# An attention kernel whose instruction order comes from a plan: refitted step lengths, a price for each pair of matmul forms, a narrower hold on VectorE, and a new order of TensorE's steps

## The chip, the cores and the metric

The kernel runs on one core of one Trainium2 chip. The metric is the device time of one execution in microseconds (us), the median over several runs. The profile calls TensorE PE (and its weight loads PEld), VectorE DVE, ScalarE ACT, GpSimd POOL and SyncE SP; a q behind a name (SPq) is the engine's queue of issued transfers.

## The reference: what is computed

Two stages in fp32. The first is attention inside chunks of 64 positions, for 8 batches, 8 heads and 576 positions. The second takes its output as x (8 batches of 576 x 512) and runs four experts, each a causal attention of width 64 over the whole sequence, of which each position uses the best two by a gate.

```
scores = scale * q_c @ k_c.T ; attn = softmax(scores) ; x = attn @ v_c     # chunks of 64
logits = x @ w_gate ; keep the 2 largest of 4, softmax over them -> w
for e in range(4):
    q, k, v = x @ wq[e], x @ wk[e], x @ wv[e]
    a = softmax(causal(scale * q @ k.T))                                    # 576 x 576
    ye = a @ v @ wo[e]
    out += w[e] * ye                                                        # for the positions that chose e
```

## The kernel before, in words

The work is cut into steps, and every step has a name, a number and an engine. A file-wide function builds them all as a graph: `add` (L85) records one step with its engine, its supposed length, what it depends on and which buffers it uses. Nothing is issued while the graph is built. Then `Plan.emit` (L142) walks through time on the host, engine by engine, with the supposed lengths, and issues each step's instructions in the order in which the walk starts them. So the lengths in the code never run on the chip; they only decide the order in which each engine's instructions stand. On the chip each engine then takes its instructions strictly in that order and waits by semaphores for data and buffers.

**TensorE's steps** are not chosen by the walk but by the table `ORDER` (L269): 372 names. They are, for the first stage, `as` (scores of a unit of one or two groups of 128 positions, L510), `at` (transposes of its softmax, L549) and `av` (times v, L570); there are 22 units. For the second stage `v` (the value projection and gate of one group, L461) and `m` (a query or key projection of one tile of 256 or 384 positions, L461; `m` 4t and 4t+1 are the queries of the two expert pairs of tile t, 4t+2 and 4t+3 the keys), `s` (scores of one row tile of one batch and expert pair, L712; `s1.2` is the third of the six steps of batch 0, pair 1), `st` (transposes of the weights, L786), `o` (weights times values, L820) and `w` (output projection of 128 positions, L850). The first four `m` and first two `v` are split into two parts, `m2` and `m2.1` being the high-order product and the two correction products. A step has one of four forms by the part of TensorE's array that its matmuls use, which the profile shows as 128*128 ("full": m, v, w), 64*128 ("rows": s, st, at), 64*64 ("quarters": as, av) and 128*64 ("cols": o).

**The other engines' steps** are taken by the walk from those that can start, the one with the smallest due time first. The due time comes from TensorE's order and is shifted by the tables `LATER` (L286, one shift per kind and engine) and `MOVED` (L293, one shift per single step). ScalarE takes the exponentials (`aa` L529, `sa` L729), copies out of PSUM (`ac` L557, `sc` L800), the high parts of x, q and k (`ax` L592, `za` L627), the values (`va` L490), half of the outputs (`y` L861) and the high parts of the weight matrices (`wh` L442). VectorE takes maxima, differences and sums of the first softmax (`ad` L520 to L535), the low parts (`ay` L594, `zd` L632 and L634), the masked scores (`sd` L722) and others. GpSimd normalises the first softmax (`ap` L538), forms the low parts of the weight matrices (`wl` L446), computes the gate and scales the second softmax (`sp` L753). SyncE issues the transfers: `lq` (K and Q of a group, L404 and L405), `lv` (V, L408), `lw` (a piece of a weight matrix, L439) and `so` (an output, L859). The very first Q goes from ScalarE's queue.

Buffers are few: 8 PSUM banks; 4 each of the K, Q and V groups; 2 each of `e` (the first softmax of a unit), `et` and `mx`; 4 of `at` (the weights of the second softmax), 2 of x.

The walk knows four things of TensorE beside a step's length: a price for a change of form (`CHANGE`, L54, by the new form alone), a stall when a new block of instructions is fetched (`fetched`, L150), a slower start (L324) and a number of filler matmuls (L325). It also knows that some VectorE and GpSimd steps get in each other's way: a VectorE step marked `port=True` is held while GpSimd is busy or has a step whose inputs are ready:

```
if held and eng == "DVE":
    if free_at["Pool"] > now or any(a.ready <= now for a in avail["Pool"]):
        continue
```

## Time and profile before

| | us |
|---|---|
| median of 3 runs | 386.13 |
| lowest and highest run | 386.06, 388.39 |
| the profiled execution | 386.02 |
| its span, first to last instruction | 384.3 |
| first matmul of a step | 4.40 |
| first matmul of av0 | 14.05 |

The granted TensorE clock is 1.0 in the profile. The views used are the page's busy times, the table of stretches (busy time of each engine in each stretch), the table of waits (who waited for whom, longest first in total, then the number of waits and the longest), the timeline (start, length, engine, line, operation, output from inputs, count; in brackets the idle time before it and what ended it) and the chain of work that ended last, in order of time (start, length, what). PE counts as busy from a matmul's start to its modelled end, so overlapping matmuls are counted once, and a weight load (PEld) can stand idle while PE is still busy.

### The profile page before, as it was taken

To read this page: it belongs to the slowest core of one execution; us is meant where nothing else is said; L and a number is where in the kernel's file an instruction comes from. 1 tells how busy PE (TensorE), PEld (TensorE's weight loads), DVE (VectorE), ACT (ScalarE), POOL (GpSimd) and SP (SyncE) were. 2 spreads that over 40 slices of the span, in tenths; PEclk is the share of its full clock that TensorE was granted. 3 is DMA by queue.
4 is the path that set the end of the run, shared out by engine and by line. 5 is a ranking of instruction groups with operands and counts; after the bars stand their busy time and mean duration, and the time that the engine had idled before them with its cause. 6 is when DMAs were issued, how large, how long until landed. Compare 5 with 4: busy or idle time off the path is not lost.

```text
span 384.3 us, 14186 instructions
## 1 busy us (share of the span) xinstructions
PE 374.5 (97%) x5602; PEld 330.2 (86%) x5603; DVE 272.1 (71%) x946; ACT 270.3 (70%) x890; POOL 170.7 (44%) x335
## 2 busy tenths in 40 slices
PE   6799999999999999999999999999999999999996
PEld 4699999898989899797997989988989889897674
DVE  3667899999489795888436779776755766668531
ACT  3564799789746965979744496798494765969651
POOL 6653255657163069455160205763705046166700
PEclk9999999999999999999999999999999999999999
DMA  8954532605252270414106126003100110000224
GB/s 286 380 200 181 195 96 78 217 3 148 77 184 93 90 245 28 163 61 139 57 29 197 53 68 239 29 3 128 67 17 15 30 58 1 2 29 3 110 84 164
DMA packets 22098, 40.76 MB, mean 106 GB/s; under 512 B 2448, under 2 KB 2704, under 8 KB 22032
## 3 DMA queue, kind: packets, MB, share of 16 engines
q1 hardware_dynamic: 21744, 39.47, 29.8%
q8 instruction: 44, 0.72, 0.8%
q10 hardware_dynamic: 288, 0.39, 0.3%
q14 instruction: 22, 0.18, 0.1%
HBM read 30.42 MB, written 9.44 MB: 104 GB/s over the span
## 4 chain that ended last, share of the span: by engine, by line
PE 92%; DMA 3%; DVE 2%; ACT 1%; issue 1%; POOL 1%; SPq 0%; POOLq 0%
PE bank L461 39%; PE bank L850 14%; PE bank L820 12%; PE bank L712 11%; PE bank L786 6%; PE bank L570 5%; PE bank L510 4%; PE bank L549 2%; DMA at<-in_wqk_dram 2%; DMA qs<-in_qt_dram 1%; POOL e L538 1%; DVE xl L594 0%; DVE e L522 0%; DVE mx L520 0%; ACT e L529 0%
## 5 line engine op out<-in xcount | busy, mean ns | idle before, releaser
L753 POOL TENSOR_SCALAR at<-at,st,gate 128x320 f32<-128x320 f32 (+4 forms) x160 | 95.0, 611 | 74.5 <-DVE st L743 49.0
L729 ACT ACTIVATE at<-at,st 128x448 f32<-128x448 f32 (+4 forms) x160 | 90.0, 601 | 0.1
L722 DVE CUSTOM_DVE_ANT_0 at<-bank,mask 128x448 f32<-128x448 f32 (+4 forms) x160 | 60.0, 425 | 12.2 <-PE bank L712 11.4
L461 PE MATMUL bank<-xh,wqk_hi 128*128 128x384 f32 (+1 forms) x208 | 65.5, 326 | 0.0
L461 PE MATMUL bank<-xl,wqk_hi 128*128 128x384 f32 (+1 forms) x208 | 65.2, 323 | 0.0
L461 PE MATMUL bank<-xh,wqk_lo 128*128 128x384 f32 (+1 forms) x208 | 65.1, 323 | 0.0
L800 ACT ACTIVATE aT<-bank 128x128 f32<-128x128 f32 (+2 forms) x256 | 57.0, 377 | 2.4 <-PE bank L786 2.0
L538 POOL TENSOR_TENSOR e<-e,mx 128x1024 f32<-128x1024 f32 (+1 forms) x21 | 34.3, 1645 | 50.1 <-DVE mx L535 28.3
L820 PE MATMUL bank<-aT,vv 128*64 128x448 f32 (+4 forms) x384 | 46.7, 392 | 0.0
L820 PEld LDWEIGHTS bank<-aT,vv 128*64 128x64 f32 x384 | 25.0, 137 | 21.8 <-issue 15.2
L764 DVE STREAM_TRANSPOSE aT<-at 32x96 f32<-32x96 f32 x128 | 34.5, 269 | 12.5 <-POOL at L753 9.0
L461 PE MATMUL bank<-wvg_hi,xh 128*128 128x260 f32 x144 | 40.5, 288 | 0.0
L461 PE MATMUL bank<-wvg_lo,xh 128*128 128x260 f32 x144 | 39.7, 283 | 0.0
L461 PE MATMUL bank<-wvg_hi,xl 128*128 128x260 f32 x144 | 39.5, 281 | 0.0
L461 PEld LDWEIGHTS bank<-xh,wqk_hi 128*128 128x128 f32 x208 | 38.2, 188 | 0.8
L461 PEld LDWEIGHTS bank<-xl,wqk_hi 128*128 128x128 f32 x208 | 38.4, 188 | 0.5 <-DVE xl L594 0.2
L461 PEld LDWEIGHTS bank<-xh,wqk_lo 128*128 128x128 f32 x208 | 38.3, 188 | 0.0
L729 ACT ACTIVATION_READ_ACCUMULATOR at<-at,st 128x1 f32 (+1 forms) x160 | 38.1, 239 | 0.0
L712 PE MATMUL bank<-kh,qh 64*128 64x288 f32 (+4 forms) x192 | 37.1, 338 | 0.0
L490 ACT ACTIVATE vv<-bank 64x260 f32<-64x260 f32 (+1 forms) x56 | 21.6, 385 | 22.0 <-PE bank L461 21.6
L712 PE MATMUL bank<-kl,qh 64*128 64x288 f32 (+4 forms) x192 | 32.8, 294 | 0.0
L786 PEld LDWEIGHTS bank<-ident,at 64*128 64x128 f32 x704 | 28.9, 139 | 3.8 <-issue 1.5
(91 smaller groups left out, 822.4 us busy)
## 6 DMA issues: line engine op xcount, KB each, us to landing
ks<-in_kt_dram SPq DMA_DIRECT2D x36, 256.0 KB, 4.7
vs<-in_vt_dram SPq DMA_DIRECT2D x36, 256.0 KB, 4.1
qs<-in_qt_dram SPq DMA_DIRECT2D x35, 256.0 KB, 5.0
out_dram<-y SPq DMA_DIRECT2D x35, 256.0 KB, 2.0
at<-in_wqk_dram SPq DMA_DIRECT2D x4, 256.0 KB, 6.4
at<-in_wvg_dram SPq DMA_DIRECT2D x2, 260.0 KB, 4.3
at<-in_wo_dram SPq DMA_DIRECT2D x2, 256.0 KB, 5.7
qs<-in_qt_dram ACTq DMA_DIRECT2D x1, 256.0 KB, 3.6
```

Of the source, the lines that this page charges most:

```text
L461: pe.matmul(bk.t[:, :n_], a, x, start=(n == 0), stop=(n == 3 * KT - 1))
L490: act.activation(v_s[b].t[p0:p0 + m, j], bk.t[r0:r0 + m, 0:W_VG], AF.Copy)
L538: o = add("DVE" if u in NORM_DVE else "Pool", 0.6 if u in NORM_DVE else 0.14 + 0.87 * G, lambda: norm.tensor_tensor(e.t[:, al], e.t[:, al] ...
L712: pe.matmul(bks[s].t[:m, :w], q[own, cs], k[own, z0 + ks.start:z0 + ks.stop], start=(x == 0), stop=(x == 2))
L722: dve.tensor_tensor_reduce(out=a.t[:r, o_ + ks.start:o_ + ks.stop], in0=bk.t[:r, :w], in1=mask[:r, m0:m0 + w], scale=1.0, scalar=first, op ...
L729: act.activation(af, af, AF.Exp, scale=-1.0, bias=st.t[:r, 0, i, 0:1], accum_out=st.t[:r, 1, i, 0:1])
L753: pool.tensor_scalar(af, af, st.t[:r, 2, i, 0:1], gt.t[:r, i, e:e + 1], op0=OP.mult, op1=OP.mult)
L764: dve.transpose(dst, src)
L786: pe.transpose(bks[r].t[:, 64 * n:64 * n + 64], a.t[own, c0:c0 + 128], ident[own, own])
L800: act.activation(dst, bks[r].t[:, n:n + 64 * m].rearrange("p (j c) -> p j c", j=m), AF.Copy)
L820: pe.matmul(bk.t[64 * s:64 * s + 64, c0 - h0:h1 - h0], vs.t[:, j, 64 * (2 * pair + s):64 * (2 * pair + s) + 64], ts[s].t[:, 448 * j + c0:4 ...
L850: pe.matmul(bk.t, up[:, k, 128 * t:128 * t + 128], wp[:, k, :], start=(n == 0), stop=(n == 5))
```

## The change

Five things are changed, all of them in the plan; no instruction is added, removed or given another shape, except that the same 372 steps stand in another order.

- `CHANGE` prices each pair of old and new form.
- The supposed lengths of TensorE's steps and of the transfers are refitted (`SCORES`, `TURNS` and single numbers).
- VectorE's step with `port=True` is held only if GpSimd is busy or has a step that could begin now, its buffers included; the test on the buffers is moved into a function `fits`.
- `ORDER` is another permutation of the 372 names. By the forms above it changes form 82 times, before 78: from full to quarters 4 (before 2), from quarters to full 9 (8), from quarters to cols 8 (7), from rows to full 6 (5), from rows to cols 6 (7), the others as before.
- `LATER` and `MOVED` have other numbers for most entries.

```
-CHANGE = {"rows": 0.15, "quarters": 0.135, "cols": 0.17, "full": 0.2}
+CHANGE = {("full", "rows"): 0.13, ("full", "quarters"): 0.133, ("full", "cols"): 0.14, ("rows", "full"): 0.236,
+          ("rows", "quarters"): 0.157, ("rows", "cols"): 0.182, ("quarters", "full"): 0.22, ("quarters", "rows"): 0.16,
+          ("quarters", "cols"): 0.16, ("cols", "full"): 0.206, ("cols", "rows"): 0.133, ("cols", "quarters"): 0.146}
...
+        def fits(o):
+            need = {}
+            for u in o.uses:
+                if u.t is None:
+                    need[id(u.pool)] = (u.pool, need.get(id(u.pool), (None, 0))[1] + 1)
+            return all(len(p) >= n for p, n in need.values())
...
-                    if free_at["Pool"] > now or any(a.ready <= now for a in avail["Pool"]):
+                    if free_at["Pool"] > now or any(a.ready <= now and fits(a) for a in avail["Pool"]):
...
-                    dur += CHANGE[o.form] if o.form != state["form"] else 0.0
+                    dur += CHANGE.get((state["form"], o.form), 0.0)
...
-as0 as1 at0 at1 av0 as3 av1 as2 v0 m1 m0 v0.1 m2 m3 v1 m3.1 m0.1 v1.1 m2.1 m1.1 at3 at2 as4 av3 av2 as5 v3 v2 m4 m6
-m7 m5 at4 at5 s0.3 av4 as6 av5 v4 m11 m10 m8 v6 s1 s0 s0.1 s0.4 s1.1 at6 s0.5 s0.2 as7 av6 v5 m9 v8 m14 st1 s1.4 st3
+as0 as1 at0 at1 av0 as2 as3 av1 v0 m2 m3 v1 m2.1 m1 m0 m1.1 m3.1 v0.1 m0.1 at2 s1.1 at3 v1.1 av2 av3 as5 as4 v2 v3
+m5 m6 m4 m7 s0.2 at4 at5 s1.2 av4 as6 av5 as9 v4 m11 v5 m8 m10 s0.1 s0.4 s0.3 at6 s0.5 s1.3 s0 as7 av6 v6 m9 m12 m14
...
-    "lw2@SP": 33.35, "lw4@SP": -61.14, "wh4@ACT": 1.19, "lw5@SP": -8.53, "wh5@ACT": -5.21, "lw6@SP": 0.21,
+    "lw2@SP": 3.31, "wh2@ACT": -1.68, "wl2@Pool": 2.15, "wh3@ACT": 9.23, "wl3@Pool": 0.2, "lw4@SP": -0.41,
...
-SCORES = {64: 0.205, 192: 0.397, 288: 0.402, 320: 0.483, 448: 0.61}
-TURNS = (0.249, 0.43)
+SCORES = {64: 0.196, 192: 0.417, 288: 0.478, 320: 0.522, 448: 0.669}
+TURNS = (0.246, 0.423)
...
-        kq_op[g] = add("dma", {0: 0.73}.get(g, 1.3), lambda: None, deps=[a], uses=[q_s[g], k_s[g]])
+        kq_op[g] = add("dma", {0: 0.73, 2: 2.4}.get(g, 1.37), lambda: None, deps=[a], uses=[q_s[g], k_s[g]])
```

Since tables of numbers set the order, three places are shown as the two built programs have them. In the new file a line's number is one higher.

The first is ScalarE at the start, from its first activation on. `wvg_hi` and `wqk_hi` are high parts of weight matrices, `e_81` and `e_82` the softmaxes of units 0 and 1, `et` copies of their transposes, `xh` the high part of x. Before:

```order
L442 ACTIVATE wvg_hi<-at_101 128x520
L529 ACTIVATE e_81<-e_81 128x256 x2
L442 ACTIVATE wvg_hi<-at_101 128x520
L529 ACTIVATE e_82<-e_82 128x256 x2
L442 ACTIVATE wqk_hi<-at_102 128x512
L442 ACTIVATE wqk_hi<-at_103 128x512
L442 ACTIVATE wqk_hi<-at_102 128x512
L557 ACTIVATE et_83<-bank_65 128x256
L557 ACTIVATE et_84<-bank_67 128x256
L592 ACTIVATE xh_87<-bank_61 128x2x128
```

Now:

```order
L443 ACTIVATE wvg_hi<-at_101 128x520
L530 ACTIVATE e_81<-e_81 128x256
L443 ACTIVATE wvg_hi<-at_101 128x520
L530 ACTIVATE e_81<-e_81 128x256
L530 ACTIVATE e_82<-e_82 128x256 x2
L443 ACTIVATE wqk_hi<-at_102 128x512
L443 ACTIVATE wqk_hi<-at_103 128x512
L558 ACTIVATE et_83<-bank_65 128x256
L443 ACTIVATE wqk_hi<-at_103 128x512
L558 ACTIVATE et_84<-bank_67 128x256
L593 ACTIVATE xh_87<-bank_62 128x2x128
```

The copy `et_83`, for which av0 waits, now stands behind two pieces of `wqk_hi` instead of three; the second half of unit 0's exponentials stands behind the second piece of `wvg_hi`.

The second is SyncE's queue at the start, from its first transfer. Before:

```order
L404 DMA ks_73<-in_kt_dram 128x512
L439 DMA at_101<-in_wvg_dram 128x520
L404 DMA ks_74<-in_kt_dram 128x512
L405 DMA qs_70<-in_qt_dram 128x512
L408 DMA vs_77<-in_vt_dram 128x512
L439 DMA at_101<-in_wvg_dram 128x520
```

Now:

```order
L440 DMA at_101<-in_wvg_dram 128x520
L405 DMA ks_73<-in_kt_dram 128x512
L409 DMA vs_77<-in_vt_dram 128x512
L405 DMA ks_74<-in_kt_dram 128x512
L406 DMA qs_70<-in_qt_dram 128x512
L440 DMA at_101<-in_wvg_dram 128x520
```

The first K (ks_73) is now issued second, and the K and Q of group 1 (ks_74, qs_70) fourth and fifth instead of third and fourth.

The third is GpSimd where it first scales the second softmax (`at`) and then normalises the next unit's first softmax (`e`). Before:

```order
L753 TENSOR_SCALAR at_102<-at_102,st_108,gate_114 128x448
L753 TENSOR_SCALAR at_102<-at_102,st_108,gate_114 128x320
L753 TENSOR_SCALAR at_102<-at_102,st_108,gate_114 128x192
L753 TENSOR_SCALAR at_102<-at_102,st_108,gate_114 64x64
L538 TENSOR_TENSOR e_82<-e_82,mx_85 128x1024
L753 TENSOR_SCALAR at_103<-at_103,st_109,gate_114 128x320
```

Now:

```order
L754 TENSOR_SCALAR at_104<-at_104,st_110,gate_114 64x64
L754 TENSOR_SCALAR at_104<-at_104,st_110,gate_114 128x576
L754 TENSOR_SCALAR at_104<-at_104,st_110,gate_114 128x448
L539 TENSOR_TENSOR e_81<-e_81,mx_85 128x512
L539 TENSOR_TENSOR e_82<-e_82,mx_86 128x1024
L754 TENSOR_SCALAR at_101<-at_101,st_107,gate_114 128x320
```

Unit 9 (the 512 wide one) now comes before unit 7 (1024 wide), because as9 now stands 13 places ahead of as7 in `ORDER` (before, 17 behind it). From there to at9, 21 places behind at8, unit 9 holds one of the two `e` buffers.

More of the change, by code (lines that the diff above doesn't have):

```diff
@@ L194, in emit @@
                         continue
-                    need = {}
-                    for u in o.uses:
-                        if u.t is None:
-                            need[id(u.pool)] = (u.pool, need.get(id(u.pool), (None, 0))[1] + 1)
-                    if any(len(p) < n for p, n in need.values()):
+                    if not fits(o):
                         continue
@@ L269 @@
 ORDER = """
-as0 as1 at0 at1 av0 as3 av1 as2 v0 m1 m0 v0.1 m2 m3 v1 m3.1 m0.1 v1.1 m2.1 m1.1 at3 at2 as4 av3 av2 as5 v3 v2 m4 m6
-m7 m5 at4 at5 s0.3 av4 as6 av5 v4 m11 m10 m8 v6 s1 s0 s0.1 s0.4 s1.1 at6 s0.5 s0.2 as7 av6 v5 m9 v8 m14 st1 s1.4 st3
-s1.2 st2 s1.3 st0 at7 s1.5 s3 as8 as9 av7 o0 m15 m13 m12 v7 s3.4 st4 st5 s3.5 st7 s3.1 s3.3 st6 s3.2 at9 at8 s2.4
-s2.5 s2.1 s2.2 s2.3 o1 av8 av9 as10 w0 m19 v10 v11 v9 m17 s2 st14 st13 st15 at10 st12 m16 m18 as11 av10 as12 o3 v12
-m21 m23 m20 st8 st9 s5.1 s5 at12 s5.4 st10 s5.2 st11 s5.5 s4.2 at11 s5.3 o2 av11 as16 as13 v13 v14 w4 m22 w3 w2 v17
@@ new lines @@
+m5 m6 m4 m7 s0.2 at4 at5 s1.2 av4 as6 av5 as9 v4 m11 v5 m8 m10 s0.1 s0.4 s0.3 at6 s0.5 s1.3 s0 as7 av6 v6 m9 m12 m14
+v8 st1 s1 st0 s1.4 st2 s1.5 st3 at7 s3.1 as8 o0 m13 m15 v7 s3 st4 st5 s3.4 st6 s3.3 st7 s3.2 at8 s2.4 s3.5 s2.1 s2.5
+o1 av8 av7 as10 w1 v12 m17 m19 v10 st12 st13 s2 s2.3 st14 s2.2 st15 at9 at10 v9 m18 v11 m16 as11 av9 av10 as12 o3
+m23 m22 m21 m20 st9 s5.1 st11 s5 s5.4 st8 s5.3 st10 at11 s5.2 s5.5 at12 o2 as15 w3 w6 v13 v14 w4 av11 av12 as13 w0
+w2 m27 m25 w5 v16 st20 s4 s4.4 st23 s4.5 st21 s4.2 st22 s4.3 s7.4 s4.1 o5 m24 v15 m26 v17 st17 st16 s7 s7.3 st19
@@ L285 @@
+m47 m44 s13 st40 s13.2 st43 s13.4 st41 s13.1 st42 s13.3 at21 s13.5 o10 av21 v31 m46 v35 m49 m51 v33 w22 v34 s12.1
+st54 s12.4 st53 s12 s12.3 st52 st55 s12.2 s15.3 s12.5 o13 w18 w21 m48 v32 m50 s15 st50 st51 s15.4 st48 s15.2 st49
+s15.1 s15.5 s14.5 s14.1 s14.3 s14.4 o12 s14 s14.2 st60 w26 w24 st62 st63 st61 w25 w23 o15 w29 st58 st56 st59 st57
+w27 w30 o14 w28 w31 w34 w33 w35 w32
 """
 LATER = {
-    "lw@SP": 276.03, "wh@ACT": 46.71, "wl@Pool": 90.36, "lq@SP": -60.46, "lv@SP": 111.48, "ad@DVE": 162.53,
@@ L288 @@
-    "aa@ACT": 88.58, "ap@DVE": 383.36, "ac@ACT": -92.93, "ac@DVE": 132.63, "ax@ACT": -48.51, "ay@DVE": -13.35,
-    "ap@Pool": -90.01, "za@ACT": 170.84, "zd@DVE": 164.23, "va@ACT": -217.77, "g@DVE": 146.79, "g@Pool":
-    -163.41, "g@ACT": -90.7, "sd@DVE": 19.06, "sa@ACT": 406.78, "sp@Pool": -302.08, "sc@ACT": -163.22, "sx@DVE":
-    177.12, "oa@ACT": -58.73, "od@DVE": -152.88, "y@DVE": -182.6, "so@SP": 220.8, "y@ACT": 334.31, "so@ACT":
-    391.64}
-MOVED = {
[29 rows of a table removed]
+    "lw@SP": 203.06, "wh@ACT": 101.31, "wl@Pool": 50.83, "lq@SP": -86.59, "lv@SP": 34.02, "ad@DVE": 125.44,
@@ L324 @@
+    "aa@ACT": 44.32, "ap@DVE": 466.25, "ac@ACT": -101.14, "ac@DVE": 193.87, "ax@ACT": -92.19, "ay@DVE": 20.02,
+    "ap@Pool": -60.4, "za@ACT": 340.99, "zd@DVE": 37.76, "va@ACT": -232.22, "g@DVE": 20.85, "g@Pool": -151.78,
+    "g@ACT": -44.96, "sd@DVE": -20.31, "sa@ACT": 431.41, "sp@Pool": -242.63, "sc@ACT": -150.03, "sx@DVE": 227.6,
+    "oa@ACT": -59.26, "od@DVE": -201.74, "y@DVE": -327.37, "so@SP": 281.34, "y@ACT": 291.82, "so@ACT": 483.43}
+MOVED = {
[26 rows of a table added]
 COLD = 7.8
 FILLS = {("as", 1): 2, ("at", 0): 9}
-SCORES = {64: 0.205, 192: 0.397, 288: 0.402, 320: 0.483, 448: 0.61}
@@ L549, in f @@
                     pe.transpose(b2[c].t[:, 64 * m:64 * m + 64], ef[own, 128 * m:128 * m + 128], ident[own, own])
-        o = add("PE", 0.01 + 0.243 * G, f, deps=[o], uses=[e, et] + b2, name=("at", u), form="rows", n_ins=16 * G + 0.3)
+        o = add("PE", 0.018 + 0.235 * G, f, deps=[o], uses=[e, et] + b2, name=("at", u), form="rows", n_ins=16 * G + 0.3)
         od = []
@@ L613, in project_qk @@
         o = project(t, 0, c1 - c0, W["wqk"], lambda w, x, k: (w.rearrange("p (m k c) -> p m k c", m=4, k=KT)[:, m, k, :], x),
-                    w_op["wqk"][m:m + 1], old, 0.143 + 5.055e-3 * (c1 - c0), [bk, xs], c1 - c0, ("m", i))
+                    w_op["wqk"][m:m + 1], old, 0.143 + 5.057e-3 * (c1 - c0), [bk, xs], c1 - c0, ("m", i))
         for b_, k0, k1, p0 in new:
@@ L824, in values @@
         deps = t_op[b, 2 * pair] + t_op[b, 2 * pair + 1] + v_op[b]
-        po = add("PE", 2.7, f, deps=deps, uses=[vs] + ts + [p[2] for p in parts], name=("o", bp), form="cols",
+        po = add("PE", 2.703, f, deps=deps, uses=[vs] + ts + [p[2] for p in parts], name=("o", bp), form="cols",
                  n_ins=48.1)
```

23 lines of the change are left out of this document (9 added, 14 removed), and 53 rows, old and new, of the table MOVED.

## Prediction

> **What bounds the kernel now.** I read the page's busy times first, then the stretches, then the waits.
>
> ```profile
> span 384.3 us, 14186 instructions
> PE 374.5 (97%) x5602; PEld 330.2 (86%) x5603; DVE 272.1 (71%) x946; ACT 270.3 (70%) x890; POOL 170.7 (44%) x335
> ```
>
> TensorE is busy 97%, no other engine above 71%. In the stretches the third number is PE's busy time:
>
> ```profile
> 0.00:16.00 16.00, 10.05 (x282) 7.26 (x283) 7.24 (x23) 7.36 (x15) 11.02 (x40) 1.00 0.90 324
> 16.00:60.00 44.00, 43.82 (x816) 42.17 (x806) 35.28 (x114) 30.83 (x90) 19.90 (x31) 1.00 0.54 189
> ...
> 300.00:360.00 60.00, 60.00 (x659) 51.96 (x647) 42.60 (x170) 46.61 (x166) 29.50 (x64) 1.00 0.08 27
> ```
>
> Only the first 16 us have room: PE stands still for 6 of them. From 16 us to the last matmul it is never idle for longer than a fraction of a microsecond. The table of waits of that stretch, PE's and then the weight loads', says how much is lost:
>
> ```profile
> PE bank L549 <- POOL e L538: 0.2, 1, 0.2
> ```
>
> ```profile
> PEld bank L820 <- issue: 15.2, 65, 0.4
> PEld bank L786 <- POOL at L753: 1.1, 3, 0.4
> PEld bank L820 <- ACT at L729: 0.7, 2, 0.4
> PEld bank L820 <- DVE st L722: 0.5, 2, 0.3
> PEld bank L570 <- ACT et L557: 0.5, 2, 0.3
> PEld bank L786 <- POOL gs L673: 0.4, 1, 0.4
> ```
>
> PE itself waits 0.2 us for another engine. Weight loads wait 3.2 us for other engines in the five rows that name one, but much of that lies under a matmul that still drains. So what an order without any wait could save behind 16 us lies between 0.2 and 3.2 us, under 1% of the run. The rest is the steps themselves, and those stay the same 372.
>
> **The start.** The chain is transfer, as0, softmax, at0, copy, av0, split into high and low, first projections. On TensorE:
>
> ```profile
> 4.40 1.13 PE L510 MATMUL bank<-ks,qs 64*64 64x64 f32 x32 [1.40 <-DMA qs<-in_qt_dram]
> 11.61 0.47 PE L549 MATMUL bank<-ident,e 64*128 64x64 f32 x8 [1.16 <-DVE e L538]
> 14.05 0.69 PE L570 MATMUL bank<-et,vs 64*64 64x64 f32 x32 [1.17 <-ACT et L557]
> 15.05 0.68 PE L570 MATMUL bank<-et,vs 64*64 64x64 f32 x32
> 16.71 1.11 PE L461 MATMUL bank<-xh,wqk_hi 128*128 128x256 f32 x8
> ```
>
> and on ScalarE and SyncE's queue:
>
> ```profile
> 8.07 0.64 ACT L442 ACTIVATE wvg_hi<-at 128x520 fp32r<-128x520 f32 x1 [0.64 <-DMA at<-in_wvg_dram]
> 11.74 1.99 ACT L442 ACTIVATE wqk_hi<-at 128x512 fp32r<-128x512 f32 x3 [1.92 <-DMA at<-in_wqk_dram]
> 13.64 0.64 ACT L557 ACTIVATE et<-bank 128x256 f32<-128x256 f32 x2
> 15.79 0.66 ACT L592 ACTIVATE xh<-bank 128x256 fp32r<-128x256 f32 x2 [0.35 <-PE bank L570]
> ```
>
> ```profile
> 0.80 0.38 SPq L404 DMA_DIRECT2D ks<-in_kt_dram  x1
> 1.23 0.42 SPq L439 DMA_DIRECT2D at<-in_wvg_dram  x1
> ```
>
> at0 starts at 11.61 and needs under half a microsecond, yet the copy `et` starts at 13.64: it stood behind three pieces of wqk_hi. In the new order it stands behind two, so by the 1.99 us for three it can start about 13.64 - 0.66 = 13.0, and av0 at 14.05 - 0.6 = 13.45. Against this, the first K is issued 1.23 - 0.80 = 0.43 us later, behind a weight piece; at the 324 GB/s of the first stretch a 256 KB transfer is 0.8 us, so as0 comes 0.4 to 0.8 us late, and at0 at 12.0 to 12.4. The second half of unit 0's exponentials now stands behind the wvg_hi that ends at 8.7; but unit 1's stand behind that piece in both orders, and unit 0's normalisation sits behind the sums of both units in VectorE's order. So the delay at at0 is K's 0.4 to 0.8, and it ends before 13.0: hidden by the wait for wqk. If the weights should land earlier than I think, it shows, up to those 0.8 us.
>
> The gain doesn't reach the projections whole. av1 now comes behind two other steps (as2, as3), av0 at 13.45 plus three steps of 0.5 = 14.95, against 15.05; the first m step needs av1's xh and came 16.71 - 15.05 = 1.66 behind it, while only v0 (half a microsecond) now stands between. That makes 16.6: **a gain of 0.1 us**. Were v0 alone what held the first m, the gain would be the whole 0.6. Bounds: -0.6 (gain) to +0.7 (K late and not hidden); I take -0.1, since xh's row at 15.79 sits on PE's.
>
> **Changes of form.** There are 82 for 78: full to quarters +2, quarters to full +1, rows to full +1, quarters to cols +1, rows to cols -1. Prices come from the chain of work, equal steps with and without a change in front:
>
> ```profile
> 67.80 2.85 PE bank L820 x24
> 85.71 2.85 PE bank L820 x24
> 90.12 0.93 PE bank L510 x64
> 91.06 1.59 PE bank L850 x6
> 107.74 1.09 PE bank L510 x64
> 136.16 1.39 PE bank L850 x6
> 137.55 2.09 PE bank L461 x12
> 139.63 2.80 PE bank L850 x12
> 184.06 1.44 PE bank L461 x12
> 353.04 3.00 PE bank L850 x12
> ```
>
> A unit's scores take 0.93 after quarters and 1.09 after full (107.74): 0.16. A w takes 1.39 after full and 1.59 after quarters (91.06): 0.20. Two w take 2.80 after full and 3.00 after rows (353.04): 0.20. The o at 67.80 follows quarters and the o at 85.71 rows, both 2.85: that swap is free. (The two L461 rows, a wide m and a v, are for later.) So 2 x 0.16 + 0.20 + 0.20 = **+0.7 us**, on the path, since PE is never idle there. It is the surest term.
>
> The Trainium skill, TensorEngine Tiling (Array Packing), Key Properties, says that changing the tiling mode drains TensorE, which speaks against this order. The rows above agree that a change is paid for, 0.16 to 0.20 us; if the rule did not hold here the sum would be 0.7 lower.
>
> **Waits that go.** Almost every step has other neighbours, so the small waits listed above have no reason to stay in their places. Bounds 0.2 and 3.2 us; a weight load's wait is lost only as far as no matmul drains above it, which puts the value nearer to PE's own row: I take **-1.0**.
>
> **Waits that come.** The new order leaves short covers at some places. s0.2 and s1.2 read queries and keys of m4 and m7. In the trace the queries of the projection just ahead of at4 (the first row below) came so:
>
> ```profile
> 37.00 0.96 PE L549 MATMUL bank<-ident,e 64*128 64x64 f32 x24
> 37.10 0.39 ACT L627 ACTIVATE qh<-bank 128x256 fp32r<-128x256 f32 x1 [1.05 <-PE bank L461]
> 37.52 0.42 DVE L632 SCALAR_TENSOR_TENSOR ql<-bank,qh 128x256 fp32r<-128x256 f32 x1 [1.01 <-ACT qh L627]
> ```
>
> The operand is ready at 37.52 + 0.42 = 37.94, 0.94 after the next step began. s0.2 has one projection between (about 1.4 us), s1.2 has s0.2, at4 and at5 (0.96 for the two transposes by the second row, and a score step): both covered, by under half a microsecond. The other place is unit 6 and 7's softmax, with unit 9's work let in between on VectorE, ScalarE and GpSimd. at6 waited before:
>
> ```profile
> 39.07 1.11 PE L510 MATMUL bank<-ks,qs 64*64 64x64 f32 x64
> 48.59 1.92 POOL L538 TENSOR_TENSOR e<-e,mx 128x1024 f32<-128x1024 f32 x1 [0.69 <-DVE mx L535]
> 55.13 5.98 POOL L753 TENSOR_SCALAR at<-at,st,gate 128x576 f32<-128x576 f32 x10 [3.71 <-ACT xh L592]
> 61.08 1.91 POOL L538 TENSOR_TENSOR e<-e,mx 128x1024 f32<-128x1024 f32 x1
> ```
>
> From as6 at 39.07 to its normalised softmax at 50.5 it is 11.4 us. The lower bound for new waits is 0.2 (as now), the upper 3.2 (as many as the weight loads show now). I take **+0.5**: about as many short covers as before, each near zero.
>
> The tail stays: the last three w and their outputs are of the same kinds in another order. The narrower hold and the refitted numbers issue nothing; they act through the order alone. SyncE's other loads move by single places and are issued far ahead.
>
> **The sum.** 386.0 for the profiled execution (its span of 384.3 and 1.7 around it): -0.1 start, +0.7 forms, -1.0 old waits, +0.5 new waits = 386.1. The median of the runs is 0.1 above that execution, so I forecast **386.2 us**, no change that can be told: about 1% (3.9 us) is what a measurement of this kernel separates from none.
>
> **Rivals.**
>
> *The waits go and none come.* Start -0.6, forms +0.7, waits -2.0, none new: 386.1 - 1.9 = 384.2. For it speaks that room is left in the start; against it that PE's own wait behind 16 us is 0.2. It is inside 1%.
>
> *TensorE's hidden room.* The weight loads wait 15.2 us for issue at L820, the o steps. If the new neighbours of o let half of that go, the time is 386.2 - 7.6 = 378.6. Against it: the two o rows above take 2.85 behind quarters and behind rows alike, so neighbours don't reach into o. Chance 0.03. The Trainium skill, Perfetto Trace Analysis, Identifying the Most-Contended Engine, holds matmul busy time for a bad measure of the room that is left and takes the weight loads' share instead, here 86%, which would leave 14%; the equal lengths of equal steps show that an order doesn't reach that room.
>
> *Unit 9 in the way: slower.* as9 takes one of two `e` buffers 13 places ahead of as7 and keeps it until at9, so units 7, 8 and 10 pass through the other, one after the other: as7, at7, as8, at8, as10, at10. Each as-to-at chain must fit under the work between. By the chain that took 11.4 us, and with the steps between as7 and at7 coming to about 13 (three projections at 1.4, two wide m at 2.1, av6 and as7 at 1, and seven short ones), the cover is 1.6 us. GpSimd's normalising of 1.9 stands behind ten scalings of 5.98, and now also unit 9's, half a unit, 1.0. If the scalings start 0.6 late as well, the cover is gone; from there each microsecond is TensorE's, at at7, at8 and at10. For over 1% it takes 1.3 us at each: 386.2 + 3.9 = 390.1. It decides only if GpSimd falls 3 us behind; it was idle 3.71 us before the ten scalings. Chance 0.05.
>
> *The order doesn't bite.* If TensorE's order were without effect on waits, the forms alone remain: 386.1 + 0.1 + 0.5 = 386.8, inside 1%.
>
> **How the numbers follow.** The forecast's own case, with small gains and losses, has 0.61; all waits gone 0.18; forms alone 0.13; unit 9 0.05; hidden room 0.03. Within 1%: 0.61 + 0.18 + 0.13 = 0.92; faster 0.03; slower 0.05. The range takes the first rival's 384.2 as its low end, and as its high end the start's loss (+0.8 against my value), no old wait gone (+1.0) and 0.6 more of new ones: 388.6. What is left out is unit 9 in full, hidden room, and the case that several bounds fall together.
>
> **What would show it.** Right: av0 at 13.4 to 13.6 and the first qk projection at 16.4 to 16.7; as0 at 4.8 to 5.2; PE busy within 1 us of 374.5; PE's own waits behind 16 us under 1 us; the span 383 to 386. The forms: PE's steps come to about half a microsecond more. Wrong: a wait of over 0.5 us at at6, at7, at8 or at10 for POOL e; an s or st step waiting for VectorE or GpSimd more than three times; a step as waiting for a transfer, which I have at nothing; or a first projection behind 17.0.

## The result, and the profile after

| | before | changed |
|---|---|---|
| median of 13 runs each | 386.50 us (385.99 to 388.69) | 389.52 us (388.91 to 390.31) |
| profiled execution | 386.02 us, span 384.3 | 389.52 us, span 387.8 |
| first qk projection / last matmul starts | 16.71 / 380.26 us | 17.35 / 383.76 us |

The ratio of the times is 1.0064 with a 95% interval of 1.0048 to 1.008: the changed kernel is slower by about 0.6%. The runs of the kernel before lie in two groups (up to 386.5 and from 387.84 on), both of which are in the ratio, and the profiled execution is of the lower one; so the two profiles differ by more, 3.5 us. The page of the changed kernel:

```profile
span 387.8 us, 14168 instructions
PE 376.6 (97%) x5602; PEld 331.1 (85%) x5603; DVE 273.9 (71%) x946; ACT 268.9 (69%) x890; POOL 170.7 (44%) x335
```

TensorE is busy 2.1 us more with the same number of matmuls, VectorE 1.8 more and ScalarE 1.4 less, GpSimd as before. The waits behind 16 us, PE's own and then those of the weight loads:

```profile
PE bank L713 <- DVE ql L633: 0.7, 1, 0.7
PE bank L462 <- DVE xl L595: 0.2, 1, 0.2
PE bank L713 <- DVE kl L635: 0.2, 1, 0.2
```

```profile
PEld bank L821 <- issue: 15.6, 67, 0.4
PEld bank L713 <- DVE ql L633: 0.8, 1, 0.8
...
PEld bank L713 <- ACT aT L801: 0.6, 3, 0.3
PEld bank L550 <- POOL e L539: 0.4, 1, 0.4
```

Before, PE's table had one row of 0.2 us. Now VectorE's low parts (`xl`, `ql`, `kl`) stand in it, and ScalarE's copies of transposed weights (`aT`) hold weight loads three times. The row that waits for issue is as before (15.6 for 15.2). The start, TensorE and then ScalarE:

```profile
5.72 1.13 PE L511 MATMUL bank<-ks,qs 64*64 64x64 f32 x32 [2.72 <-DMA ks<-in_kt_dram]
...
8.18 1.13 PE L511 MATMUL bank<-ks,qs 64*64 64x64 f32 x32 [0.37 <-DMA qs<-in_qt_dram]
...
13.02 0.46 PE L550 MATMUL bank<-ident,e 64*128 64x64 f32 x8 [1.17 <-DVE e L539]
...
14.23 0.69 PE L571 MATMUL bank<-et,vs 64*64 64x64 f32 x32
...
17.35 1.21 PE L462 MATMUL bank<-xh,wqk_hi 128*128 128x256 f32 x8
```

```profile
13.49 0.38 ACT L558 ACTIVATE et<-bank 128x256 f32<-128x256 f32 x1 [0.79 <-PE bank L550]
```

as0 comes 1.3 us later than before (5.72 for 4.40), at0 1.4 later (13.02 for 11.61), and the copy `et` no longer stands behind weight pieces but waits for at0 itself.

**Where the 3.5 us are.** The last matmul starts 3.50 later: 0.64 at the first qk projection, and 2.86 in the stretch from there to the last matmul (383.76 - 17.35 = 366.41 for 380.26 - 16.71 = 363.55). At the 0.17 us a change that `forms_plus` shows below, the four more changes of form are 0.7 of the 2.86, and about 2.2 is left for waits. (A fit over all steps of both traces, with one length for each kind of step and one price for each kind of change, from one step's first matmul to the next one's, gives the changes less, 0.3 to 0.4, and the waits 2.4 to 2.5. So the split is good to a few tenths.) By that fit the largest waits of the changed kernel are s5 0.88, m11 0.49 and st0 0.44, and some twelve of 0.1 to 0.2 follow; before, the largest are m11 and s1.1, 0.25 each. "The stretch" below is this time; it leaves the start out.

### The profile page after: what moved, and what is told of

It is laid out like the page before. It is cut to its first block, busy times and chain, and to the rows that moved or that the text cites. A ratio compares the mean times of both kernels' runs of the same rounds, so it can differ in the third digit from the quotient of the medians.

```text
span 387.8 us, 14168 instructions
## 1 busy us (share of the span) xinstructions
PE 376.6 (97%) x5602; PEld 331.1 (85%) x5603; DVE 273.9 (71%) x946; ACT 268.9 (69%) x890; POOL 170.7 (44%) x335
## 4 chain that ended last, share of the span: by engine, by line
PE 87%; DVE 6%; ACT 4%; DMA 1%; issue 1%; SPq 0%; POOL 0%; POOLq 0%; DVEq 0%; ACTq 0%
PE bank L462 35%; PE bank L851 14%; PE bank L821 11%; PE bank L713 11%; PE bank L787 6%; PE bank L571 4%; PE bank L511 4%; PE bank L550 2%; ACT at L730 2%; DMA qs<-in_qt_dram 1%; DVE mx L532 1%; DVE aT L765 1%; ACT xh L593 1%; DVE e L523 1%; DVE xl L595 1%
## 5 line engine op out<-in xcount | busy, mean ns | idle before, releaser
L754 POOL TENSOR_SCALAR at<-at,st,gate 128x576 f32<-128x576 f32 (+4 forms) x160 | 95.0, 610 | 66.1 <-DVE st L744 51.1
L730 ACT ACTIVATE at<-at,st 128x576 f32<-128x576 f32 (+4 forms) x160 | 90.9, 622 | 0.9 <-DVE st L723 0.9
L723 DVE CUSTOM_DVE_ANT_0 at<-bank,mask 128x320 f32<-128x320 f32 (+4 forms) x160 | 60.5, 425 | 11.7 <-PE bank L713 9.9
L821 PEld LDWEIGHTS bank<-aT,vv 128*64 128x64 f32 x384 | 25.0, 137 | 21.6 <-issue 15.6
L730 ACT ACTIVATION_READ_ACCUMULATOR at<-at,st 128x1 f32 (+1 forms) x160 | 41.5, 260 | 0.0
L595 DVE TENSOR_TENSOR xl<-bank,xh 128x256 fp32r<-128x256 f32 (+1 forms) x58 | 24.8, 480 | 11.6 <-ACT xh L593 11.3
```

Source lines behind the costliest of these rows:

```text
L595: x_part[t].append((c0, c0 + w, add("DVE", dve_t(2 * w), lambda x=x, part=part: dve.tensor_tensor(x(1), part(), x(0).bitcast(F32), op=OP.s ...
L723: dve.tensor_tensor_reduce(out=a.t[:r, o_ + ks.start:o_ + ks.stop], in0=bk.t[:r, :w], in1=mask[:r, m0:m0 + w], scale=1.0, scalar=first, op ...
L730: act.activation(af, af, AF.Exp, scale=-1.0, bias=st.t[:r, 0, i, 0:1], accum_out=st.t[:r, 1, i, 0:1])
L754: pool.tensor_scalar(af, af, st.t[:r, 2, i, 0:1], gt.t[:r, i, e:e + 1], op0=OP.mult, op1=OP.mult)
L821: pe.matmul(bk.t[64 * s:64 * s + 64, c0 - h0:h1 - h0], vs.t[:, j, 64 * (2 * pair + s):64 * (2 * pair + s) + 64], ts[s].t[:, 448 * j + c0:4 ...
```

## The experiments

Times are medians; the kernel before ran beside each group on the same chip. Ratios are to it, and aren't quotients of the two medians.

### Are the waits the program's, or chance?

`before_again` and `after_again` are the two kernels once more.

> The kernel before once more, for the scatter of its start: if the first projection's time is set by transfers, as0 and the first projection move by up to half a microsecond between two executions of the same program (16.7 in the first one), while the waits behind 16 us recur at the same steps (m11, s1.1) with a sum of 0.9 plus or minus 0.3 us.

> The changed kernel once more: the first projection within half a microsecond of 17.35, and the same three waits for VectorE (s5 0.9, m11 0.5, st0 0.4 us, each plus or minus 0.15) with a sum of 3.0 plus or minus 0.4 us behind the start. If the waits were chance, they stand at other steps or are gone.

Measured: 386.44 and 389.84 us. First qk projection 17.04 and 17.40; stretch 363.69 and 366.71. Before, m11 and s1.1 wait 0.26 and 0.25 again; changed, s5 0.89, st0 0.43, and m11 0.81 (more than expected, 0.49 the first time). So the waits belong to the program, though not each one's size. The start of one program moves between executions: the first qk projection by 0.3 us, and as1 and at0 by 0.7 (7.48 and 12.36 in `before_again`, 6.79 and 11.61 before).

### The start

Four kernels move the loads and copies of the first 15 us, two from each side. `k_first` is the changed kernel with the first K issued ahead of the first weight piece again; `start_old` gives it the whole old order K, weights, K, Q, V. `k_second` is the kernel before with the weight piece ahead of K; `wh_two` is the kernel before with the copy `et` ahead of the third `wqk_hi`, which is what the change did on ScalarE.

```
k_first:  -            nc.sync.dma_start(k_s[g].t, kt[g])
          +            if g:
          +                nc.sync.dma_start(k_s[g].t, kt[g])
          ...
          +                    if first:
          +                        nc.sync.dma_start(k_p[0], kt[0])
wh_two:   +                    if piece == 1:
          +                        late.append(go)
          ...
          +                    if u == 0:
          +                        late.pop()()
```

> The changed kernel with two rows of SyncE's queue swapped: the first K ahead of the first piece of wvg, as before; every other row of every engine as in the changed kernel. Theory 1 (K's place in the queue makes as0 late, and in the new order nothing hides it): as0 at 4.3 to 4.6 instead of 5.72, at0 at 11.5 to 11.8, the first qk projection at 16.2 to 16.8 instead of 17.35, the run 0.6 to 1.2 us under the changed kernel, 388.3 to 388.9. Rival (the whole stream of transfers was late by chance in the profiled execution, K's place is worth only its 0.43 us of issue and hides behind the wait for wqk): as0 at 5.0 to 5.3 and the run within 0.3 us of 389.5.

> The changed kernel with five rows of SyncE's queue as before: K of group 0, the piece of wvg, K and Q of group 1, then V of group 0; every other row of every engine as in the changed kernel. In the runs so far at0 comes 4.8 us behind as1 and not behind as0, since the first softmax is normalised behind the sums of both units. Theory 1 in its new form (as1, so the landing of group 1's Q, sets the start): as1 at 6.7 to 7.2, at0 at 11.5 to 12.0, av0 0.4 behind the second piece of wqk_hi or 1.2 behind at0, the first qk projection at 16.1 to 16.6, the run 0.4 to 0.8 us under k_first, 388.0 to 388.4. Rival (as0 alone matters): as k_first, 388.8, the first qk projection at 16.8.

> The kernel before with the two first rows of SyncE's queue swapped: the first piece of wvg ahead of the first K; every other row as before. Theory 1 with cover (the wait of the copy et behind three pieces of wqk hides the late K): as0 at 5.5 to 5.8, at0 at about 13.0, av0 at 14.0 to 14.5, the run 0 to 0.4 us over before. Rival without cover: av0 as late as as0, 15.4, the run 1.3 us over before, 387.4.

> The kernel before with one thing of the changed one: on ScalarE the copy et of unit 0 stands ahead of the third piece of wqk_hi; every other row as before. Theory (the copy's place is worth what the prediction said, and in the old order the two steps behind av1 cover xh): av0 at 13.4 to 13.6 instead of 14.05, the first qk projection 0.4 to 0.6 earlier at 16.1 to 16.3, the run 385.5 to 385.8. Rival (xh of av1 or the late third piece holds the first projection anyway): within 0.1 of before.

| | as0 | as1 | at0 | av0 | first qk | time, ratio and interval |
|---|---|---|---|---|---|---|
| before | 4.40 | 6.79 | 11.61 | 14.05 | 16.71 | |
| changed | 5.72 | 8.18 | 13.02 | 14.23 | 17.35 | 389.52, 1.0064 (1.0048 to 1.008) |
| k_first | 4.35 | 7.84 | 12.68 | 13.89 | 16.84 | 388.85, 1.0055 (1.0036 to 1.0073) |
| start_old | 4.27 | 6.90 | 11.92 | 14.24 | 17.20 | 389.20, 1.0063 (1.0042 to 1.0084) |
| k_second | 5.60 | 7.85 | 12.65 | 14.49 | 17.15 | 387.92, 1.0006 (0.9986 to 1.0026) |
| wh_two | 4.34 | 6.77 | 11.57 | 13.56 | 16.88 | 386.52, 1.0001 (0.998 to 1.0021) |

`k_first` missed at0 (11.5 to 11.8 expected): as0 is back at 4.35, but at0 follows as1 by 4.8 to 5.0 us in every line of the table, because the normalisation of unit 0 stands behind the sums of both units on VectorE; and as1 waits for the second Q. `k_second` came as expected: as0 at 5.60, av0 at 14.49, so in the old order most of the late K is covered. `start_old` brings at0 back, and missed the projections (16.1 to 16.6 expected), for the next transfer is late instead. ScalarE, then TensorE in it:

```profile
13.28 0.63 ACT L452 ACTIVATE wqk_hi<-at 128x512 fp32r<-128x512 f32 x1 [2.28 <-DMA at<-in_wqk_dram]
13.82 0.37 ACT L567 ACTIVATE et<-bank 128x256 f32<-128x256 f32 x1
```

```profile
14.24 0.69 PE L580 MATMUL bank<-et,vs 64*64 64x64 f32 x32 [1.13 <-ACT et L567]
```

`wh_two` gets the copy's gain at av0 (13.56) and loses it to the next step, which waits for Q until 14.74:

```profile
14.74 0.69 PE L517 MATMUL bank<-ks,qs 64*64 64x64 f32 x32 [0.49 <-DMA qs<-in_qt_dram]
```

So every order of these loads leads to a first projection of 16.7 to 17.4. In these rows what is gained at one transfer is lost at another; but each order has one profiled execution, and as1 moves by 0.7 us between two executions of one program, so how much of it is the order is not shown. The start costs the changed kernel 0.4 to 0.6 us, and it is not what makes it slower by 3.

### The price of a change of form

`forms_plus` is the kernel before with ten full steps issued behind the next transposes instead of ahead of them. No row of another engine moves. (The expectation names scores as the steps in between; they are the transposes `st`.)

```
+                if eng == "PE" and o.name in BEHIND:
+                    kept = (BEHIND[o.name], o.fn)
...
+BEHIND = {("m", 14): ("st", 1), ("m", 20): ("st", 8), ("m", 24): ("st", 18), ("v", 18): ("st", 28), ...}
```

> The kernel before, with ten of TensorE's full steps (m14, m20, m24, v18, m32, v26, w14, m40, v35, m50) issued behind the next step of scores instead of ahead of it; nothing else is moved on any engine. That makes 20 more changes of form, ten from rows to full and ten from full to rows. If a change costs TensorE what the refitted table says (0.24 and 0.13 us, 0.37 a pair), TensorE's last step ends 3 to 4.2 us later and the time is 389.3 to 390.4 us against 386.1. If the price is hidden or is an artefact of the fit, the time stays within 0.5 us of the kernel before.

Measured: 393.07 us, ratio 1.0152 (1.0124 to 1.0179): more than expected. One of the ten places, m20 and st8, before:

```profile
119.21 0.33 PE L461 MATMUL bank<-xh,wqk_hi 128*128 128x384 f32 x1
...
121.12 0.34 PE L461 MATMUL bank<-xh,wqk_lo 128*128 128x384 f32 x1
121.39 0.91 PE L786 MATMUL bank<-ident,at 64*128 64x64 f32 x22
122.10 0.34 PE L712 MATMUL bank<-kh,qh 64*128 64x192 f32 x2
```

and with m20 between the two transposes:

```profile
121.13 0.34 PE L469 MATMUL bank<-xh,wqk_lo 128*128 128x384 f32 x1
121.40 0.46 PE L794 MATMUL bank<-ident,at 64*128 64x64 f32 x8
121.79 0.44 PE L469 MATMUL bank<-xh,wqk_hi 128*128 128x384 f32 x1
...
124.08 0.66 PE L794 MATMUL bank<-ident,at 64*128 64x64 f32 x14
124.54 0.34 PE L720 MATMUL bank<-kh,qh 64*128 64x192 f32 x2
```

Before, m20 and the transposes take 122.10 - 119.21 = 2.89; now 124.54 - 121.40 = 3.14, and the step ahead ends 0.27 behind its last start instead of 0.17. That is 0.35 for one pair, and all ten places show 0.34 or 0.35: 3.45 us, 0.17 a change. At these ten places the price is true, and no work hides it. They test changes between rows and full alone; of those that the new order adds only one is of these (rows to full), four have quarters on one side, and one from rows to cols goes. The Trainium skill, TensorEngine Tiling (Array Packing), Key Properties, says that a change of mode drains TensorE, and the ten places agree that it is paid for. The rest of the 7.1 us by which the last matmul came later is not forms: 1.7 is the start, under a lowered clock (last section), and some 2.0 is waits: the stretch is 368.97, 5.4 above 363.55. Ten steps of TensorE out of their places, with the other engines' orders as they were, cost as much in waits as the change did.

### Which engine do the waits wait for?

`sx_one_after` is the changed kernel with a quarter of VectorE's corner transposes of the weights; `sc_quarter_after` and `sc_quarter_before` let ScalarE copy only a quarter of each block of transposed weights. All three leave that part of the second softmax's transposition out.

```
sx: -            for r in range(2):
    +            for r in range(1):
sc: -    act.activation(dst, bks[r].t[:, n:n + 64 * m].rearrange(...), AF.Copy)
    +    act.activation(dst[:, :, 0:16], bks[r].t[:, n:n + 64 * m].rearrange(...)[:, :, 0:16], AF.Copy)
```

> The changed kernel with one of the four corner transposes of each weights tile left out three times in four (VectorE does 32 of 128; the corners stay zero, so the weights are not complete), order otherwise the same. VectorE has 25 us less to do. Theory 2 (the waits that came are the low parts of q, k and x late in VectorE's queue, behind these transposes and behind sums): the waits at st0 with s1.4 (0.44) and s5 (0.87) vanish, TensorE's waits behind 18 us fall by 1.0 to 2.0 us, the run 387.5 to 388.5. Rival (TensorE's own neighbours are too close, whatever VectorE has to do): those two waits stay and the run falls by under 0.4 us.

> The changed kernel with ScalarE's copies of the transposed weights cut to a quarter of their columns (the rest of the weights stays zero), order the same; the same cut is made to the kernel before in sc_quarter_before. Theory 3 (most of the new small waits in the stretches of s and st are PSUM banks that come back late because ScalarE is behind with these copies): TensorE's waits behind the start fall by 1.0 us or more against the changed kernel, and by 0.3 or less in the kernel before. Rival (the waits hang on VectorE): they fall by under 0.5 us, and about alike in both.

> The kernel before with ScalarE's copies of the transposed weights cut to a quarter of their columns (the rest stays zero), order the same. Theory 3: TensorE's waits fall by 0.3 us or less, the run 385.6 to 386.2. Rival: they fall as much as in sc_quarter_after.

Measured: `sx_one_after` 389.16 us, ratio 1.005 (1.0032 to 1.0068), stretch 366.00: the waits of s5 and st0 are gone, as expected, but m11's is 0.77 (in the range of the two executions of the changed kernel, 0.49 and 0.81) and small ones come elsewhere, so a cut of three quarters buys 0.4 us where 1 to 2 were expected. `sc_quarter_after` 387.00 us, 0.9998 (0.9979 to 1.0017), stretch 363.87, down 2.54. `sc_quarter_before` 385.40 us, 0.9963 (0.9941 to 0.9985), stretch 362.24, down 1.31, more than the 0.3 expected of it. In `sc_quarter_after` the `aT` rows are gone from the waits, while those for VectorE are the same to 0.1:

```profile
PE bank L713 <- DVE ql L633: 0.7, 1, 0.7
PE bank L462 <- DVE xl L595: 0.3, 1, 0.3
PE bank L713 <- DVE kl L635: 0.2, 1, 0.2
```

So of the 2.2 us, 2.54 - 1.31 = 1.2 hangs on ScalarE's time in these copies, in many small pieces. That it acts through PSUM banks given back late is read from the `aT` rows and not shown apart: with the copies cut, ScalarE's other work comes sooner too. About 1 us net is left, and VectorE's low parts still stand there, 1.8 us at three places (s5, m11, st0) against small waits of the old order that went. Taking two of the three away (`sx_one_after`) bought less than their size, so that part is argued more than shown. s5 is one of them, VectorE and then TensorE of the changed kernel:

```profile
125.50 1.11 DVE L765 STREAM_TRANSPOSE aT<-at 32x96 f32<-32x96 f32 x4
126.62 0.62 DVE L633 SCALAR_TENSOR_TENSOR ql<-bank,qh 128x192 fp32r<-128x192 f32 x2
```

```profile
127.30 0.25 PE L713 MATMUL bank<-kh,qh 64*72 64x64 f32 x1 [0.70 <-DVE ql L633]
```

VectorE makes four transposes first, and TensorE needs the low part behind them.

### Tables or lengths?

The change has two halves: the tables (order of TensorE and shifts of the others) and the numbers that the plan walks with. `old_tables_new_model` has the old tables with all new numbers, `new_tables_old_model` the reverse. `scores_only` and `rest_only` split the new numbers on the old tables, `scores_288` takes one number alone, `after_old_scores` gives the changed kernel the old lengths of the score steps.

```
scores_only:      -SCORES = {64: 0.205, 192: 0.397, 288: 0.402, 320: 0.483, 448: 0.61}
                  +SCORES = {64: 0.196, 192: 0.417, 288: 0.478, 320: 0.522, 448: 0.669}
scores_288:       -SCORES = {64: 0.205, 192: 0.397, 288: 0.402, 320: 0.483, 448: 0.61}
                  +SCORES = {64: 0.205, 192: 0.397, 288: 0.478, 320: 0.483, 448: 0.61}
after_old_scores: -SCORES = {64: 0.196, 192: 0.417, 288: 0.478, 320: 0.522, 448: 0.669}
                  +SCORES = {64: 0.205, 192: 0.397, 288: 0.402, 320: 0.483, 448: 0.61}
```

> The old order of TensorE's steps and the old shifts of due times (ORDER, LATER, MOVED), with the refitted lengths, the new prices of form changes and the narrower hold. 78 changes of form again, K first again. Theory (the loss comes with the new order and its tables): 385.5 to 387.0. Rival (the refitted lengths by themselves move the other engines' steps to worse places): 388.5 or more.

> The changed kernel's three tables (order, later, moved) with the old step lengths, the old prices of a change of form and the old hold rule. The theory that the tables and the lengths belong together, and that any mismatch of the other engines' instructions with TensorE's order costs waits: 389.5 us or more, with waits of TensorE behind the start at or above the changed kernel's 3.0 us. The rival, that the refitted lengths alone put the other engines' instructions in the wrong places: 388 us or less, waits below 1.5 us and only the forms' 0.7 and the start's half a microsecond left.

> The kernel before with the refitted lengths of the score steps alone (the five numbers of SCORES); tables, the other lengths, prices of forms and the hold stay old. If the score steps' longer lengths are what moves the other engines' instructions, TensorE's stretch from the first qk projection to its last matmul grows by 1.2 to 2 us over the 363.6 of the kernel before, and the time is 387.3 to 388. If it is the other lengths, the stretch stays within 0.4 us of 363.6.

> The kernel before with all the refitted numbers and the narrower hold except the lengths of the score steps, tables old. The counterpart: if the score steps' lengths are the cause, the stretch stays within 0.4 us of 363.6; if the others are, it grows by 1.2 to 2 us. If both of the pair grow, no single number is the cause: any shift of the supposed times against the tables brings waits.

> The kernel before with one number changed, the supposed length of the 288 wide score steps (0.402 to 0.478, the largest relative shift of the five, for two of a pair's six steps). If that one carries the waits, the stretch is 364.8 or more (363.6 before, 365.6 with all five); if the shift is spread over the five, it is 364.2 or less.

> The changed kernel with the old lengths of the score steps, all else as changed. If the longer lengths as such put VectorE's and ScalarE's instructions in worse places, the stretch from the first qk projection to the last matmul falls from 366.5 to 365.3 or less and the time to 388.5 or less. If tables and lengths have to match, whichever they are, the stretch grows by 1 us or more and the time to 390.5 or more.

| | tables | score lengths | other numbers | time | ratio (interval) | stretch |
|---|---|---|---|---|---|---|
| before | old | old | old | 386.1 to 387.4 | | 363.55 |
| rest_only | old | old | new | 385.78 | 0.9985 (0.997 to 0.9999) | 363.06 |
| scores_288 | old | one new | old | 388.26 | 1.004 (1.002 to 1.006) | 365.52 |
| scores_only | old | new | old | 389.75 | 1.0078 (1.0057 to 1.01) | 365.58 |
| old_tables_new_model | old | new | new | 388.85 | 1.0043 (1.0024 to 1.0063) | 365.30 |
| changed | new | new | new | 389.52 | 1.0064 (1.0048 to 1.008) | 366.41 |
| after_old_scores | new | old | new | 394.10 | 1.0185 (1.0161 to 1.0209) | 371.18 |
| new_tables_old_model | new | old | old | 399.20 | 1.0327 (1.0299 to 1.0354) | 368.74 |

My theory for `old_tables_new_model` (the loss comes with the new order, so 385.5 to 387) fell: with TensorE's order untouched, the new numbers alone bring 1.8 us of waits. `scores_only` and `rest_only` show which: the score lengths, all of it. The other numbers act on little: `rest_only` moves 9 of ScalarE's instructions and 9 of VectorE's against the kernel before, `scores_only` 61 and 37 (the time of `scores_only` is above the 387.3 to 388 expected, since its start fell under a lowered clock; its stretch, +2.0, is as expected). The stretch of `rest_only` is 0.5 us shorter than before, a little more than the 0.4 allowed for. `scores_288` shows that a single one carries it, 0.402 to 0.478 us. And `after_old_scores` shows that the longer lengths are not bad as such: with the old ones in the new tables the time rises by 4.6 us more, as the theory that tables and lengths have to match expected. About 1.7 of the 4.8 by which its profiled stretch grows is a clock of 0.50 between 360.6 and 364.0 us (last section), behind the first wait below; its two runs at a full clock, 393.40 and 394.27 us, are nearly as slow without it. PE's waits in it:

```profile
PE bank L787 <- POOL at L754: 1.6, 1, 1.6
PE bank L550 <- POOL e L539: 1.3, 1, 1.3
PE bank L713 <- DVE ql L633: 0.7, 1, 0.7
```

`new_tables_old_model` loses 7 us more in the start, where GpSimd's first normalisation (unit 1's) now stands behind a row of weight splits, and where the clock is 0.50 from 17.2 to 24.0 us:

```profile
17.39 1.26 POOL L442 TENSOR_TENSOR wqk_lo<-at,wqk_hi 128x512 fp32r<-128x512 f32 x1 [1.45 <-ACT wqk_hi L438]
18.61 1.05 POOL L534 TENSOR_TENSOR e<-e,mx 128x512 f32<-128x512 f32 x1
```

```profile
19.71 0.69 PE L545 MATMUL bank<-ident,e 64*128 64x64 f32 x8 [6.03 <-POOL e L534]
```

**How one number reaches TensorE.** `scores_288` has the steps of TensorE and the transfers of SyncE in the same order as before. Buffer numbers aside, 49 of ScalarE's 890 instructions, 29 of VectorE's 946 and 3 of GpSimd's 335 stand a few places elsewhere. One of them can be followed. ScalarE, VectorE and TensorE before, around 60 us:

```profile
57.15 0.44 ACT L729 ACTIVATE at<-at,st 128x192 f32<-128x192 f32 x1
...
57.59 1.05 ACT L529 ACTIVATE e<-e 128x1024 f32<-128x1024 f32 x1
```

```profile
58.67 1.22 DVE L531 TENSOR_REDUCE mx<-e 128x16 f32<-128x1024 f32 x1
...
61.72 0.56 DVE L634 TENSOR_TENSOR kl<-bank,kh 128x384 fp32r<-128x384 f32 x1
```

```profile
62.74 0.42 PE L786 MATMUL bank<-ident,at 64*128 64x64 f32 x6
```

and with the one number changed:

```profile
57.21 0.44 ACT L729 ACTIVATE at<-at,st 128x192 f32<-128x192 f32 x1
...
57.65 0.44 ACT L729 ACTIVATE at<-at,st 128x192 f32<-128x192 f32 x1
...
58.09 1.05 ACT L529 ACTIVATE e<-e 128x1024 f32<-128x1024 f32 x1
```

```profile
59.17 1.22 DVE L531 TENSOR_REDUCE mx<-e 128x16 f32<-128x1024 f32 x1 [0.53 <-ACT e L529]
60.59 0.22 DVE L632 SCALAR_TENSOR_TENSOR ql<-bank,qh 128x64 fp32r<-128x64 f32 x1 [0.19 <-ACT qh L627]
...
62.50 0.56 DVE L634 TENSOR_TENSOR kl<-bank,kh 128x384 fp32r<-128x384 f32 x1
```

```profile
63.21 0.46 PE L786 MATMUL bank<-ident,at 64*128 64x64 f32 x8 [0.40 <-DVE kl L634]
```

One exponential of 0.44 us has moved ahead of a unit's softmax on ScalarE. VectorE, which takes its rows in order, waits 0.53 for it and 0.19 for the next; `kl` comes 0.78 later, and TensorE stands for 0.40. A score step is 0.08 us longer in the plan, and TensorE loses five times that at this place.

### Fillers ahead of at0

`fill_before` and `fill_after` issue three more filler matmuls ahead of at0, to close TensorE's idle time there.

```
+        for _ in range(2 if len(calls) in (5, 8, 11) else 1):
```

> The kernel before with three more filler matmuls of 0.22 us ahead of at0 (12 for 9), the planned order of everything else unchanged. If the upper group of its times (387.2 to 389) comes from a lower granted clock behind TensorE's idle time in the start, nearly all runs lie at 385.8 to 386.8 and the mean falls by half a microsecond or more. The rival, that the upper group has another cause (late transfers): the share of runs above 387 stays at a third or more.

> The changed kernel with the same three more fillers. Its runs show one group (388.9 to 390.3) and the profiled ones a full clock, so by the theory of the clock nothing changes: median 389.5 within 0.4. If the fillers run into at0's time, it grows by up to half a microsecond.

Measured: 386.50 us, ratio 1.0002 (0.9988 to 1.0017), 3 of 12 runs above 387 us, with a granted clock of 0.95 to 0.996, beside 9 of 21 of the kernel before, all with 0.996; and 389.33 us, 1.008 (1.0065 to 1.0094). So the upper group does come with a lowered clock (the last section counts it over all runs), but the fillers didn't do away with it, and 3 of 12 isn't told apart from 9 of 21. The changed kernel stays where it was, as expected.

## Why the prediction was wrong

386.2 us was forecast with a range to 388.6; it is 389.5, a loss inside 1%, where no change had been expected. The 1% that the prediction took for the least that a measurement can tell was too coarse: the interval of the ratio is 0.3% wide and clear of one. By the prediction's own terms:

- **Start, -0.1: measured +0.64** (+0.4 between the second executions). I let the first K alone delay at0 (12.0 to 12.4 forecast, 13.02 measured). I took either the 0.43 us of the issue or the 0.8 of the transfer ahead of it for K's delay; as0 is 1.3 late, near the two together. And I did not cost group 1's Q, which stands one place later in SyncE's queue. By `k_first` it is this Q, through as1, that sets at0. The 0.6 from the copy didn't reach the projections: in `wh_two` the next Q stands in its place.
- **Changes of form, +0.7: right as far as tested.** `forms_plus` gives 0.17 a change between rows and full, 0.7 for four; the fit makes it less, 0.3 to 0.4.
- **Waits that go, -1.0, and waits that come, +0.5: the step that failed.** Together they were put at -0.5 and are about +2.2. "The small waits listed above have no reason to stay in their places" is true of the new order and says nothing of its sum; `forms_plus` shows that mere displacement costs 2.0. Of the new waits I looked for short covers of operands on TensorE's side only. Those at s0.2 and s1.2 held, as forecast. What came late was work behind ScalarE's copies (1.2) and low parts in VectorE's queue, at s5 and st0 behind its transposes; the prediction names neither.
- **"The narrower hold and the refitted numbers issue nothing; they act through the order alone"**: true, but taken for nothing. The order in question is also VectorE's and ScalarE's, and one of the numbers moved it for 2 us with TensorE's left alone. The hold is indeed nothing: with the old rule in the changed kernel, the plan puts every engine's instructions in the same order.
- **Rivals.** Unit 9 in the way: no, though its 390.1 lies nearest to the measured time; that is luck. The waits for GpSimd's `e` come to 0.4 on the weight loads and none on PE. TensorE's hidden room: no, 15.6 for 15.2. All waits go, and the order that doesn't bite: the reverse of what happened. A rival was missing that puts the loss on the orders of VectorE and ScalarE.

The prediction's own list of signs tells it: as0 at 5.72 (4.8 to 5.2 was right), av0 at 14.23 (13.4 to 13.6), PE busy for 376.6 (within 1 us of 374.5), its own waits behind 16 us 1.1 (under 1), the first projection behind 17.0, and score and transpose steps that wait for VectorE.

What stays open: why the new tables with the numbers they go with are 2 us worse in waits than the old pair. The runs show that tables with score lengths which aren't theirs are worse than with their own (in the stretch the old ones by 1.8 to 2.0, the new ones by 2.3 and, without the piece at a lowered clock, about 3.1), not why one matched pair is better than the other.

## What to carry to other kernels

Where a plan's supposed lengths decide the order of in-order engines, a number that is nearer to the chip is not a harmless edit: it is a new order on every engine, and its orders have to be compared place by place before it is called free. Cost a reordering by who gives back buffers and operands late (PSUM banks behind copies, low parts behind long vector work), not by TensorE's neighbours alone; and take the waits of a displaced order as a loss of its own size, here 2 us in 386 three times over. Of the variants that do all the work none beats the kernel before by more than 0.15% (`rest_only`, all new numbers but the score lengths), and part of that may be its clock: one of its 10 runs has a lowered one, beside 9 of 21.
